# Block attention and two expert layers on one core: lookup tables built on the chip, and a new hand-written order of all steps

## The chip, the core and the metric

The kernel runs on one core of a Trainium2 chip. The metric is the time of one execution in microseconds (us), taken on the device. Engines are named as the profile names them: PE is the matrix engine, PEld its weight load, DVE the vector engine, ACT the scalar (activation) engine, POOL the GpSimd engine, and SP the engine on whose queue all transfers from and to memory are issued.

## What is computed

```python
# attention: q, k, v of shape (2, 8, 768, 64); block = 32, window = 16
k_sum = k.reshape(B, H, nb, block, D).max(axis=3)
v_sum = v.reshape(B, H, nb, block, D).mean(axis=3)
scores_l = scale * np.matmul(q, k.transpose(0, 1, 3, 2))        # kept where |i - j| < window, else -1e9
scores_s = scale * np.einsum('bhsd,bhnd->bhsn', q, k_sum) + np.log(block)
a = softmax(concatenate([scores_l_masked, scores_s]))            # 768 local + 24 block columns
attn = np.matmul(a, concatenate([v, v_sum]))
# x: (1536, 512), two expert layers with d_ff = 2048
h = x @ w_in;  g = h * np.clip(h + 3.0, 0.0, 6.0) / 6.0;  x = g @ w_out
h = x @ w2_in; out = (h * sigmoid(h)) @ w2_out
```

## The kernel before, in words

The 1536 tokens are two batches of 768. **Attention** works in 24 units, two for each of 12 groups of 128 queries. For a group, `scores` multiplies 64-row windows of q with 96 local keys and the 24 block maxima; `masked` (DVE) adds the mask table and takes the row minimum; `exps` and `guard` (ACT) make the exponentials and their sum; `inverse` (DVE) and `normal` (POOL or DVE) divide; `turn` (PE) transposes and `turned` (ACT or DVE) copies out; `mix` (PE) multiplies with a window of v that `load_v` brings from memory and whose last 24 rows `v_put` fills with block means; `mixed_hi` and `mixed_lo` split the result into two parts x = hi + lo. Before that, `load` brings k, q and v; `par` (first batch of k) sorts token parity, `tr` transposes on PE against the identity matrix `ident`, `k_copy`, `q_copy` and `k_max` take the result out of PSUM, and `keys` (POOL or DVE) lays out the window of keys. The block maxima span a whole batch, so no score of a batch can be made before all k of it has come; the block means likewise need all v of a batch.

**The expert layers** keep the precision of float32 by splitting both operands in two float32r parts and making three products. A weight tile of 128 rows is brought by `fetch` (512 KB, the first half of a pair w_in, the second w_out) and split by `conv_top` (ACT or DVE), `conv_join` (DVE), `conv_hi` (ACT or DVE) and `conv_lo` (POOL or DVE). `hidden i p` is half a step of the first product (6 matmuls of 512 columns, `p` is 0 or 1), `act`, `gate`, `gate_hi`, `gate_lo` make the activation and its two parts, and `project i p` is half a step of the second product. The first 24 steps of `hidden` work on blocks of 512 tokens; the very first block is tokens 0 to 511, which are attention groups 0 to 3 (units 0 to 7). Later steps use sums of products (`prod`, `prodb`, `ssum`, `tsum`, `c11` and the like), which save PE work and cost DVE work.

**The order** is one written table, `ORDER`: 1961 entries that are issued in this order, each on the engine of its function, so that each engine has a fixed list that it works through without overtaking. A `*` behind an entry puts a copy or subtraction on DVE that would otherwise be on ACT or POOL (`copier`, and `eng` in `normal`, `keys`, `conv_lo`). Buffers are taken from rings in the order of the table. `rouse` and `warm` are matmuls whose results nobody reads; they lie in the gaps of PE in the first microseconds.

The table `cst` holds the identity matrix (128 columns), a matrix for the block means (48 columns) and three masks (360 columns). Before, the host makes it in `shape_constants`, and `table 0` and `table 1` (line 1177) bring it from memory in two transfers of 88 and 180 KB. It is used by `tr` and `turn` (L500, L675), `v_sums` (L551), `v_rows` (L566) and `masked` (L633). Lines that the prediction speaks of: `fetch` L416 and L418, `load` L458 and L473, `par` L486, `scores` L618, `exps` L647, `normal` L667, `mix` L689, `mixed_hi` L711, `mixed_lo` L715, `hidden` L731, first-layer `project` L808. In the changed kernel these lines are 14 less.

## Time and profile before

| what | value |
|---|---|
| median of 3 runs (lowest to highest) | 586.29 us (584.81 to 587.84) |
| the profiled execution's own time | 586.36 us |
| its span in the profile | 584.6 us |
| granted PE clock over the span | 0.997 of full |
| busy over the span: PE, DVE, ACT, POOL | 97%, 79%, 45%, 14% |
| moved from and to memory | 47.81 MB read, 3.15 MB written |

How to read it: the span is measured from the first instruction to the last, and the profiled execution's own time has 1.8 us around it. Matmuls are pipelined and their ends are modelled, so the start of one to the start of the next says how long it held PE, and a busy share of PE is not a share of useful work. All engines work through their lists in order, so a wait of one instruction holds back everything behind it on that engine.

### The profile page before, as it was taken

To read this page: it belongs to the slowest core of one execution; us is meant where nothing else is said; L and a number is where in the kernel's file an instruction comes from. 1 tells how busy PE (TensorE), PEld (TensorE's weight loads), DVE (VectorE), ACT (ScalarE), POOL (GpSimd) and SP (SyncE) were. 2 spreads that over 40 slices of the span, in tenths; PEclk is the share of its full clock that TensorE was granted. 3 is DMA by queue.
4 is the path that set the end of the run, shared out by engine and by line. 5 is a ranking of instruction groups with operands and counts; after the bars stand their busy time and mean duration, and the time that the engine had idled before them with its cause. 6 is when DMAs were issued, how large, how long until landed. Compare 5 with 4: busy or idle time off the path is not lost.

```text
span 584.6 us, 9610 instructions
## 1 busy us (share of the span) xinstructions
PE 569.9 (97%) x3624; PEld 481.0 (82%) x3624; DVE 460.9 (79%) x1033; ACT 263.3 (45%) x614; POOL 81.1 (14%) x88
## 2 busy tenths in 40 slices
PE   8789999999999999999999999999999999999997
PEld 7677788888888888888888887888888898888886
DVE  3699986687749898998999999748987686757764
ACT  4797784544142416243446474524445134424220
POOL 1253314140001100001100402002010000111000
PEclk9998999999999999999999999999999999999999
DMA  9998896222001103224121111131322211220013
GB/s 225 237 213 211 222 247 168 64 43 83 36 1 36 40 33 109 72 76 139 39 73 36 37 36 43 67 108 50 94 73 81 100 37 36 73 61 13 0 73 144
DMA packets 70094, 51.57 MB, mean 88 GB/s; under 512 B 38432, under 2 KB 64544, under 8 KB 70048
## 3 DMA queue, kind: packets, MB, share of 16 engines
q1 hardware_dynamic: 70048, 50.97, 32.4%
q8 instruction: 28, 0.46, 0.3%
q14 instruction: 18, 0.15, 0.1%
HBM read 47.81 MB, written 3.15 MB: 87 GB/s over the span
## 4 chain that ended last, share of the span: by engine, by line
PE 85%; DVE 8%; DMA 2%; ACT 2%; SPq 1%; issue 1%; POOL 0%; DVEq 0%; POOLq 0%
PE bank L1035 26%; PE bank L808 23%; PE bank L811 21%; PE bank L731 10%; PE bank L689 2%; DMA stage<-in_v_dram 1%; PE bank L675 1%; PE bank L618 1%; DMA early_w<-in_q_dram 1%; DVE r L1082 1%; DVE bits L435 1%; SPq L458 1%; DVE values L1082 1%; SPq L473 1%; ACT early_units L647 1%
## 5 line engine op out<-in xcount | busy, mean ns | idle before, releaser
L808 PE MATMUL bank<-g,w 128*128 128x512 f32 x432 | 105.5, 392 | 0.0
L811 PE MATMUL bank<-w,g 128*128 128x512 f32 (+1 forms) x429 | 101.2, 385 | 0.0
L808 PEld LDWEIGHTS bank<-g,w 128*128 128x128 f32 x432 | 79.9, 188 | 16.4 <-issue 0.4
L811 PEld LDWEIGHTS bank<-w,g 128*128 128x128 f32 x429 | 79.5, 188 | 16.0
L450 POOL TENSOR_TENSOR w<-bits,w 128x512 fp32r<-128x512 f32 x25 | 36.2, 1454 | 288.0 <-ACT w L446 216.4
L1035 PE MATMUL bank<-w,x 128*128 128x512 f32 (+1 forms) x360 | 74.2, 348 | 0.9 <-DVE x L1018 0.6
L1035 PEld LDWEIGHTS bank<-w,x 128*128 128x128 f32 x360 | 59.2, 189 | 10.4 <-DVE r L1060 0.8
L1035 PE MATMUL bank<-x,w 128*128 128x512 f32 (+1 forms) x240 | 49.4, 348 | 0.0
L731 PE MATMUL bank<-x,w 128*128 128x512 f32 x192 | 46.8, 395 | 0.5 <-DVE stat L633 0.5
L1035 PEld LDWEIGHTS bank<-x,w 128*128 128x128 f32 x240 | 39.3, 189 | 5.8
L731 PEld LDWEIGHTS bank<-x,w 128*128 128x128 f32 x192 | 35.4, 188 | 8.5 <-DVE stat L633 0.9
L426 ACT CAST top<-words 128x512 f16<-128x512 bf16 x46 | 35.8, 778 | 12.6 <-DVE cst L435 3.7
L435 DVE SCALAR_TENSOR_TENSOR bits<-words,top 128x512 uint32<-128x512 uint32 x49 | 36.0, 734 | 4.9 <-ACT top L426 4.0
L762 ACT ACTIVATE values<-values 128x512 f32<-128x512 f32 x39 | 24.3, 627 | 34.0 <-DVE values L1076 20.0
L811 PE MATMUL bank<-w,w 128*128 128x512 f32 (+1 forms) x159 | 39.4, 386 | 0.0
L788 DVE TENSOR_TENSOR g<-values,g 128x512 fp32r<-128x512 f32 x46 | 31.6, 686 | 7.1 <-ACT g L782 6.5
L808 PE MATMUL bank<-w,w 128*128 128x512 f32 x144 | 36.5, 391 | 0.0
L811 PEld LDWEIGHTS bank<-w,w 128*128 128x128 f32 x159 | 29.4, 188 | 5.8
L808 PEld LDWEIGHTS bank<-w,w 128*128 128x128 f32 x144 | 26.8, 188 | 5.4
L1035 PE MATMUL bank<-w,w 128*128 128x256 f32 (+1 forms) x144 | 28.5, 337 | 0.7 <-DVE r L1082 0.7
L446 ACT CAST w<-bits 128x512 fp32r<-128x512 f32 x30 | 18.5, 620 | 22.6 <-DVE bits L435 14.7
L1082 DVE TENSOR_TENSOR values<-bank,values 128x512 f32<-128x512 f32 x37 | 25.3, 687 | 3.3 <-PE bank L1035 2.4
(193 smaller groups left out, 971.5 us busy)
## 6 DMA issues: line engine op xcount, KB each, us to landing
words<-in_moe_w_out_dram SPq DMA_DIRECT2D x32, 511.8 KB, 3.3
words<-in_moe_w_in_dram SPq DMA_DIRECT2D x32, 511.0 KB, 3.8
early_w<-in_q_dram SPq DMA_DIRECT2D x12, 256.0 KB, 5.3
out_dram<-acc SPq DMA_DIRECT2D x11, 256.0 KB, 2.0
early_r<-in_v_dram SPq DMA_DIRECT2D x13, 192.0 KB, 4.5
stage<-in_k_dram SPq DMA_DIRECT2D x3, 512.0 KB, 5.2
stage<-in_v_dram SPq DMA_DIRECT2D x3, 512.0 KB, 7.4
early_w<-in_k_dram SPq DMA_DIRECT2D x6, 256.0 KB, 5.6
```

Of the source, the lines that this page charges most:

```text
L426: copier("conv_top", h)(out=top[:, 1], in_=src[:, 2])
L435: nc.vector.scalar_tensor_tensor(out=bitss.take(h, bit_users(h)), in0=rest, scalar=13, in1=tops.use(h).bitcast(U32), op0=ALU.logical_shift ...
L446: copier("conv_hi", h)(out=w_half(h, 0), in_=bitss.use(h).bitcast(F32))
L450: eng.tensor_tensor(out=w_half(h, 1), in0=bitss.use(h).bitcast(F32), in1=w_half(h, 0).bitcast(F32), op=ALU.subtract,)
L689: nc.tensor.matmul(ps[D * e : D * e + D, o : o + QW], v[:NSLOT, h * D : (h + 1) * D], own(pTs, 2 * n + e)[:NSLOT, hp * P + QW * w : hp * P ...
L731: nc.tensor.matmul(ps[:, :n], w[:, a, kk * P : (kk + 1) * P], x[:, o // SUB : (o + n) // SUB, b, kk, :], start=(m == 0), stop=(m == last),)
L762: nc.scalar.activation(out=r, in_=ps, **kind)
L788: eng.tensor_tensor(out=g[:, 1, cols], in0=r[:, cols], in1=g[:, 0, cols].bitcast(F32), op=ALU.subtract)
L808: nc.tensor.matmul(ps[:, o : o + n], lhs, g[:, b, shift : shift + n], **flags)
L811: nc.tensor.matmul(ps[:, : len(cols)], g[:, a, rows], rhs, **flags)
L1035: nc.tensor.matmul(ps, lhs(a, kk), rhs(b, kk), start=(i == 0), stop=(i == 5))
L1082: nc.vector.tensor_tensor(out=out, in0=banks.use(("prod", p, k)), in1=r, op=ALU.add)
```

## The change

Three things change. The two transfers of the table are gone; the host's table is a single zero that nobody reads. In their place POOL makes the table with three new steps: `diagonal` (a memset and an affine select), `masks` (a memset, two affine selects, two copies, three memsets) and `means` (a memset, two affine selects). And the table `ORDER` is another one: 1962 entries, the same steps with the same counts apart from the tables, in another order, with 213 instead of 195 entries marked `*`.

```diff
-    c[:, :P] = np.eye(P)
-    c[np.arange(P), Z0 + 16 + np.arange(P) // 16] = 1.0 / BLOCK
-    return c
+    return np.zeros((1, 1), np.float32)
...
 ORDER = """
-zero, grow 6, grow 9, rouse 6, rouse 11, rouse 5, rouse 9, load k 0 0, par k 0 1, rouse 4, table 0, rouse 10,
+zero, rouse 11, rouse 3, load k 0 0, par k 0 0, rouse 8, rouse 5, rouse 10, clear, load k 0 2, rouse 1,
...
-    def table(part):
-        cols = slice(0, M0) if part == 0 else slice(M0, NCONST)
-        nc.sync.dma_start(out=cst[:, cols], in_=consts[:, cols])
+    def diagonal():
+        nc.gpsimd.memset(ident, 0.0)
+        nc.gpsimd.affine_select(
+            out=ident,
+            in_=ident,
+            compare_op=ALU.not_equal,
+            fill=1.0,
...
+    def band(t, expr, base, sign, fill):
+
+        nc.gpsimd.affine_select(
+            out=t, in_=t, compare_op=ALU.is_ge, fill=fill, base=base, pattern=expr,
+            channel_multiplier=sign,
+        )
+
+    def means():
+
+        t = cst[:, Z0:M0]
+        nc.gpsimd.memset(t, 1.0 / BLOCK)
+        band(t, [[-16, M0 - Z0]], 256, 1, 0.0)
+        band(t, [[16, M0 - Z0]], -241, -1, 0.0)
+
+    def masks():
+
+        wide = kws[0][:, : LOC + QW]
+        nc.gpsimd.memset(wide, 0.0)
+        band(wide, [[1, LOC + QW]], -1, -1, -1e9)
+        band(wide, [[-1, LOC + QW]], 2 * WINDOW - 1, 1, -1e9)
+        view = cst[:, M0:].rearrange("p (m n) -> p m n", m=3)
+        for rows, o in ((slice(0, QW), 0), (slice(QW, P), QW)):
+            nc.gpsimd.tensor_copy(
+                out=view[rows, :, :LOC],
+                in_=wide[rows, o : o + LOC].unsqueeze(1).to_broadcast([QW, 3, LOC]),
+            )
+        nc.gpsimd.memset(view[:QW, 0, :PAD], -1e9)
+        nc.gpsimd.memset(view[QW:, 2, LOC - PAD : LOC], -1e9)
+        nc.gpsimd.memset(view[:, :, LOC:], math.log(BLOCK))
```

**The start of SP's queue.** Names: `stage` takes k and v of the first batch, `early_w` with `in_q_dram` or `in_k_dram` a quarter of a batch's q or k, `cst` the table, `words` a weight tile. Before:

```order
L458 DMA stage_80<-in_k_dram 128x8x128
L1177 DMA cst<-in_consts_dram 128x176
L458 DMA stage_81<-in_k_dram 128x8x128
L458 DMA stage_82<-in_k_dram 128x8x128
L473 DMA early_w_88<-in_q_dram 128x8x64 x2
L1177 DMA cst<-in_consts_dram 128x360
L473 DMA early_w_88<-in_q_dram 128x8x64 x2
L458 DMA stage_83<-in_v_dram 128x8x128
L473 DMA early_w_88<-in_k_dram 128x8x64 x2
L458 DMA stage_83<-in_v_dram 128x8x128
L458 DMA stage_84<-in_v_dram 128x8x128
```

and now:

```order
L444 DMA stage_80<-in_k_dram 128x8x128
L444 DMA stage_81<-in_k_dram 128x8x128
L444 DMA stage_82<-in_k_dram 128x8x128
L459 DMA early_w_88<-in_q_dram 128x8x64 x4
L444 DMA stage_83<-in_v_dram 128x8x128 x2
L444 DMA stage_84<-in_v_dram 128x8x128
L459 DMA early_w_88<-in_k_dram 128x8x64 x2
L402 DMA words_69<-in_moe_w_in_dram 128x4x511
L404 DMA words_70<-in_moe_w_out_dram 128x2047
L459 DMA early_w_88<-in_q_dram 128x8x64 x2
```

The two transfers of the table are gone, and the first transfer of the second batch's k stands behind all three of v instead of behind the first.

**PE around the first `hidden`.** The tiles `x_0` are the first 512 tokens, `bank` with `cst` on the right a transposition (`tr` or `turn`), `early_g`/`early_units`/`early_r` on the right alone a `mix`. Before, from the last row of one `scores` of a later group (the last `mix` of the first 512 tokens stands ten rows ahead of it):

```order
L618 MATMUL bank_74<-early_units,early_w_89 64x120 x2
L731 MATMUL bank_75<-x_0_64,w_87 128x512 x12
L500 MATMUL bank_76<-cst,early_w_88 128x128 x4
L675 MATMUL bank_79<-cst,early_units 120x128 x4
L500 MATMUL bank_72<-cst,early_w_88 128x128 x4
L731 MATMUL bank_78<-x_0_64,w_441 128x512 x12
L731 MATMUL bank_73<-x_0_64,w_442 128x512 x12
```

and now:

```order
L675 MATMUL bank_78<-early_g_96,early_r_97 64x64 x16
L486 MATMUL bank_77<-cst,early_w_88 128x128 x4
L717 MATMUL bank_76<-x_0_64,w_87 128x512 x6
L717 MATMUL bank_73<-x_0_64,w_86 128x512 x12
L486 MATMUL bank_72<-cst,early_w_88 128x128 x4
L486 MATMUL bank_75<-cst,early_w_88 128x128 x4
L717 MATMUL bank_76<-x_0_64,w_87 128x512 x6
L486 MATMUL bank_79<-cst,early_w_88 128x128 x4
L486 MATMUL bank_78<-cst,early_w_88 128x128 x4
L717 MATMUL bank_74<-x_0_64,w_327 128x512 x6
```

Now the first `hidden` stands directly behind one transposition after the last `mix`, and the second batch's first transpositions, which stood ahead of it, stand between the halves of the next ones.

**POOL's start.** `top`, `kT` and `early_r` are cleared first in both; `cst` is the table, and `ISA` with the line of the next instruction is a reload of POOL's library. Now:

```order
L1227 MEMSET early_r_97 96x512
L1162 MEMSET cst 128x128
L1163 ISA
L1163 AFFINE_SELECT cst<-cst 128x128
L1190 MEMSET early_w_95 128x160
L1175 AFFINE_SELECT early_w_95<-early_w_95 128x160 x2
L1195 COPY cst<-early_w_95 64x3x96 x2
L1199 MEMSET cst 64x16
L1200 MEMSET cst 64x16
L1201 MEMSET cst 128x3x24
L579 COPY early_w_95<-kT_98 128x4x96
```

Before, the copy of `keys` (L593) followed the clearing of `early_r` at once, and the reload stood ahead of the first `normal` (L667).

## Rows read from the trace of the kernel before

**Rows 1.** Page of the profile: busy us, share of the span, number of instructions.

```profile
PE 569.9 (97%) x3624; PEld 481.0 (82%) x3624; DVE 460.9 (79%) x1033; ACT 263.3 (45%) x614; POOL 81.1 (14%) x88
```

**Rows 2.** Timeline of PE, 44 to 110 us: start, duration, line, out<-in, [idle before <-releaser].

```profile
45.56 1.71 PE L618 MATMUL bank<-early_w,early_w 64*64 64x120 f32 x32 [1.34 <-DVE early_w L527]
...
48.24 1.57 PE L689 MATMUL bank<-early_g,early_r 120*64 120x64 f32 x32
...
50.33 1.05 PE L618 MATMUL bank<-early_units,early_w 64*64 64x120 f32 x32
51.31 3.02 PE L731 MATMUL bank<-x,w 128*128 128x512 f32 x12
54.17 0.60 PE L500 MATMUL bank<-cst,early_w 128*128 128x128 f32 x4
54.60 0.60 PE L675 MATMUL bank<-cst,early_units 128*120 128x128 f32 x4
...
58.85 3.04 PE L731 MATMUL bank<-x,w 128*128 128x512 f32 x12 [0.45 <-DVE stat L633]
...
67.37 1.15 PE L689 MATMUL bank<-early_units 120*64 120x64 f32 x32
68.46 3.01 PE L808 MATMUL bank<-g,w 128*128 128x512 f32 x12
...
77.16 5.62 PE L731 MATMUL bank<-x,w 128*128 128x512 f32 x24
```

**Rows 3.** Chain of waits, whole span: start, duration, what it went through.

```profile
250.15 16.32 PE bank L808 x72
```

**Rows 4.** Waits of PE after 100 us: us in total, times, longest.

```profile
PE bank L1035 <- DVE r L1082: 0.7, 1, 0.7
PE bank L1035 <- DVE x L1018: 0.6, 1, 0.6
```

**Rows 5.** Chain of waits followed back from 60 us: start, duration, what it went through.

```profile
0.74 0.42 SPq L458
...
5.06 6.12 DMA early_w<-in_q_dram
...
15.66 7.51 DMA stage<-in_v_dram
...
25.37 0.58 ACT early_units L576
...
28.02 1.53 ACT early_units L647 x8
...
29.56 0.21 ACT stat L658
...
36.64 0.20 DVE early_units L633
...
37.25 0.60 DVE kmax L514
...
49.87 0.59 ACT x L711
...
50.48 0.69 DVE x L715
```

**Rows 6.** Stretches of 10 us: stretch, length, busy us (instructions) by engine, PE clock, DMA share, GB/s.

```profile
30.00:40.00 10.00, 8.50 (x164) 7.31 (x162) 9.16 (x48) 9.88 (x39) 5.16 (x7) 1.00 1.15 196
40.00:50.00 10.00, 8.43 (x130) 6.96 (x127) 9.14 (x31) 7.90 (x38) 8.05 (x15) 0.83 1.08 251
50.00:60.00 10.00, 9.55 (x77) 7.64 (x76) 9.41 (x39) 7.71 (x27) 0.00 (x0) 1.00 0.81 204
```

**Rows 7.** Timeline of POOL, 0 to 40 us: start, duration, instruction, [idle before <-releaser].

```profile
1.46 0.52 POOL L1203 MEMSET early_r<- 96x512 f32 x1
11.96 0.50 POOL L593 COPY early_w<-kT 128x384 f32<-128x384 f32 x1 [9.97 <-ACT kT L508]
...
24.45 0.99 POOL L667 TENSOR_TENSOR early_units<-early_units,stat 128x480 f32<-128x480 f32 x1 [0.70 <-DVE stat L662]
```

More of the change, by code (lines that the diff above doesn't have):

```diff
@@ L153 @@
-q_copy 1 2 1, conv_hi 9, load_v 14, mix 6, scores 9, keys 21, turn 17, mixed_hi 6, turned 17, conv_lo 7*,
-load_v 15, gate_lo 3, project 3 0, conv_top 12*, conv_join 12, project 3 1, grow 0, conv_hi 12, mixed_lo 6,
-masked 19, exps 19, mix 7, mixed_hi 7, conv_lo 12, mixed_lo 7, hidden 6 0, keys 20, fetch 13, conv_top 13*,
-hidden 6 1, conv_join 13, load_v 16, gate_hi 5*, conv_hi 13*, normal 16, turn 16, turned 16*, conv_lo 13*,
-guard 19, hidden 14 0, inverse 19, normal 19*, hidden 14 1, fetch 14, conv_top 14, conv_join 14, conv_hi 14*,
@@ L158 @@
-gate_hi 4, gate_lo 4, masked 18, load_v 17, act 6, hidden 11 0, hidden 11 1, act 11, fetch 11, conv_top 11,
-act 14, project 2 1, gate 6, gate 11, turn 19, mix 8, conv_lo 14, fetch 15, gate 14, exps 18, conv_join 11,
-fetch 19, scores 10, keys 22*, conv_top 15*, gate_lo 5, guard 18, conv_lo 9, project 4 0, load_v 19,
-inverse 18, turned 19, normal 18, mixed_hi 8, load_v 18, mixed_lo 8, masked 21, hidden 13 0, gate_hi 6*,
-hidden 13 1, act 13, conv_join 15, gate 13, grow 5, turn 18, turned 18*, gate_lo 6, exps 21, guard 21,
@@ new lines @@
+masked 10, mixed_lo 0, load_v 6, turned 7, masked 11, keys 9, turned 5*, grow 9, load_v 7, keys 8, scores 4,
+exps 10, masked 9, turn 4, conv_lo 1, mix 3, turned 4, masked 8, load_v 5, mixed_lo 1, mixed_hi 3, mixed_lo 3,
+load_v 4, mix 2, mixed_hi 2, mixed_lo 2, tr k 1 2 0, conv_lo 2, hidden 1 0, conv_top 6*, conv_join 6,
+guard 10, conv_hi 6*, exps 8, guard 8, fetch 4, conv_top 4*, conv_join 4, conv_hi 4*, exps 11, guard 11,
+conv_lo 6*, inverse 10, inverse 8, load k 1 1, conv_lo 4*, exps 9, hidden 0 0, hidden 0 1, normal 10,
@@ new lines @@
+v_sums 1 0, gate_hi 0*, load_v 10, tr q 1 1 0, exps 12, tr q 1 1 1, turn 9, gate_hi 2*, guard 12, hidden 3 0,
+hidden 3 1, masked 13, keys 16, turned 9, fetch 5, gate_lo 0, gate_lo 1, conv_lo 3*, q_copy 1 1 0, exps 13,
+inverse 12, normal 12*, load v 1 2, normal 11, guard 13, project 0 0, load v 1 1, grow 1, inverse 13,
+normal 13, act 3, gate 3, turn 11, fetch 7, turned 11*, q_copy 1 1 1, conv_top 5, conv_join 5, masked 15,
+project 1 0, turn 12, scores 8, masked 14, turn 13, masked 16, masked 17, v_pair 1 1, project 0 1, exps 15,
@@ new lines @@
+project 2 1, gate_lo 4, turn 17, turned 17, scores 9, keys 20*, masked 19, masked 18, exps 19, load_v 17,
+keys 21*, mix 7, mixed_hi 7*, load_v 16, mix 8, conv_lo 12, exps 18, hidden 6 0, hidden 6 1, guard 18,
+mixed_lo 7, hidden 10 0, mixed_hi 8*, guard 19, hidden 10 1, act 6, inverse 18, normal 18*, gate 6,
+mixed_lo 8, act 10, gate 10, hidden 11 0, hidden 11 1, conv_hi 9, conv_lo 9*, inverse 19, act 11, gate 11,
+grow 0, turn 18, gate_hi 6*, normal 19, gate_lo 6, fetch 13, conv_top 13, project 4 0, conv_join 13,
@@ new lines @@
+conv_hi 13*, fetch 14, conv_top 14*, turn 19, turned 19, scores 10, masked 20, exps 20, conv_lo 13*,
+hidden 14 0, hidden 14 1, masked 21, exps 21, conv_join 14, guard 20, keys 22*, project 4 1, conv_hi 14*,
+act 14, conv_lo 14*, guard 21, keys 23, inverse 20, fetch 11, conv_top 11*, normal 20*, conv_join 11,
+conv_hi 11, gate 14, hidden 13 0, gate_hi 5, gate_lo 5, hidden 7 0, hidden 7 1, act 7, load_v 18, inverse 21,
+hidden 13 1, project 6 0, conv_lo 11, gate 7, act 13, gate 13, fetch 15, turned 18, load_v 19, mix 9,
@@ new lines @@
+load_v 21, conv_top 15*, turn 20, turned 20, normal 21, scores 11, hidden 8 0, grow 2, project 6 1,
+mixed_hi 9*, masked 22, exps 22, conv_join 15, conv_hi 15*, conv_lo 15, gate_hi 7, gate_lo 7, gate_hi 10,
+turn 21, guard 22, turned 21*, tsum 0 3 0, mixed_lo 9, project 5 0, project 7 0, hidden 12 0, hidden 12 1,
+hidden 8 1, inverse 22, masked 23, exps 23, guard 23, load_v 20, normal 22, hidden 15 0, t_hi 0 3 0,
+t_lo 0 3 0, act 8, gate 8, finish 0 0 0 0, mix 10, load_v 23, mixed_hi 10, mixed_lo 10, hidden 15 1,
```

395 lines of the change are left out of this document (187 added, 208 removed).

## Prediction

> **What bounds the kernel now.** I read the page first: PE is busy 97% of the span and every other engine less than 80% [rows 1]. So the end moves only with microseconds in which PE does nothing useful, and the next question is where those are. The timeline of PE answers it. The first `hidden` starts at 51.31 us, and from there matmuls follow one another with few gaps, such as 0.45 us ahead of 58.85 [rows 2]; after 100 us the waits of PE that the trace names are a few of 0.4 to 0.7 us [rows 4]. The reader should see that from about 77 us on there is next to nothing to win, and that the start is where PE time is lost.
>
> How much is lost there comes from counting. The price of a PE step is its start to the next start: a half step of `hidden` or `project` 1.36 us (72 matmuls in 16.32, so 6 in 1.36 [rows 3]), a transposition (`tr`, `turn`) 0.43 to 0.44, `scores` 0.98, `mix` 1.09 [rows 2]. Ahead of the first `hidden` the order of before has 20 `tr`, 11 `turn`, 8 `scores`, 4 `mix` and the sums over v (2.8 us, the same in both kernels): 31 x 0.44 + 8 x 0.98 + 4 x 1.09 + 2.8 = 28.6 us of useful work. It starts at 51.3, so **22.7 us are lost**. At 77.16, when step 4 of `hidden` starts, the useful work ahead of it is 53.5 us by the same prices (28.6, then 14 half steps, 7 turns, 4 `tr`, 2 `mix` and so on), so the loss has grown to 23.7. `rouse` and `warm` count as loss. The rest of the loss is a few microseconds up to the end, and the tail (the last products and their stores) stands in the same order in both.
>
> What sets 51.3? The chain of waits shows it: transfers until 23.2 us (q until 11.2, the last v until 15.66 + 7.51 = 23.17), then ACT and DVE in turn until `mixed_hi` at 49.87 and `mixed_lo` at 50.48 [rows 5]. The stretches agree: from 30 to 60 us DVE is busy 9.1 to 9.4 of 10 us and ACT 7.7 to 9.9 [rows 6]. **The start is bound by transfers for about 23 us and by ACT and DVE after that.**
>
> **The change, part by part. The transfers.** The table is 0.27 MB. The last v is the end of 4.99 MB in the order of before and came at 23.17, so 4.99 / (23.17 - 0.74) = 0.222 MB per us, with 0.74 the first issue [rows 5]. Now 4.19 MB stand up to the last v: 19.6 us. But PE's list has the second batch's first k next, before `scores 3` of the first; it is the end of 4.72 MB, 22.0 us. PE then needs two `tr` halves, the row of block means and a `turn` before `scores 3`, about 2.4 us: 24.4, against the 25.37 at which ACT's chain behind the same point started [rows 5]. Gain at this point: **about 1 us**. Up to the last window of v that the first 512 tokens need, the queue holds 9.40 MB instead of 9.68: weights (2 MB) and the second batch's k are still ahead, so what is named as being put off is put off by little. At 0.222 that is 43.1 us instead of 44.3, no later than ACT needs.
>
> **ACT up to the first `hidden`.** This term sets the start. First the method on the kernel before: from 25.37 [rows 5] to its last `mixed_hi` of the first 512 tokens ACT has 8 `exps` (1.53), 7 `guard` (0.2), 16 copies (0.58) and 2 `conv_top` (0.75): 12.2 + 1.4 + 9.3 + 1.5 = 24.4, which gives 49.8; it ended at 49.87 + 0.59 = 50.5. So ACT ran with 0.7 us of waits. Now: q's second quarter is transposed at 22.9, its copy ends at 23.5, an `exps` and a `guard` end at 25.2, and then come 6 `exps`, 5 `guard`, 15 copies, 1 `conv_top`: 9.2 + 1.0 + 8.7 + 0.75 = 19.65. That is 44.9; with the same 0.7 of waits 45.6, and `mixed_lo` (0.6 to the next issue [rows 5]) makes 46.2. DVE has 17 us in that time and is no bound, and POOL 12. **The first `hidden` starts near 46.2 instead of 51.3.** But the work ahead of it on PE is less as well: 16 `tr`, 8 `turn`, 6 `scores`, 4 `mix`, the v sums: 23.6 us. Loss: 46.2 - 23.6 = **22.6, against 22.7**. Five microseconds earlier, with five microseconds of work put off: by itself it gains nothing.
>
> **What was put off.** From the first `hidden` to step 4 PE now has 57.6 - 23.6 = 34.0 us of work, DVE 32.9 and ACT 29.7 by the prices above (before: 24.9, 18.9, 18.4). All is nearly in balance, so PE is not covered with ease. I walked it: the three halves of `hidden` to 50.3, the second batch's `tr` (their q can be issued only when a k buffer is free, at about 46, and lands near 50), step 2 at 53.5 (its `conv_lo` ends on POOL near 51), two `scores` near 57 to 59 behind a key copy of ACT that ends near 56.5, `project 0` at 63.5 behind `gate_lo` at 63.3, step 1 of it 0.4 late behind `conv_lo` on DVE, step 4 at 80.1 to 81. Loss there: 22.5 to 23.4, I take 22.9, against 23.7: **-0.8 us**.
>
> **The tables on POOL.** 13 short instructions. No row shows an affine select; the nearest rows bound one between 0 and the 0.99 of a 480-column multiplication, and a 512-column memset took 0.52 [rows 7]; I take 0.3, nearest the memset for 128 and 160 columns. Ten stand ahead of the first `keys`, at most 9.9 us from 1.98, so 11.9; POOL was idle until 11.96 before [rows 7], and `masked` needs the masks after 14. The identity is two of them, at most 2.0, so ready by 4.0, ahead of the first transposition (near 7, after k has landed and been sorted). Cover: POOL's idle time, of which even the upper price uses no more than there was. **0**. What it costs if the cover is gone is a rival below.
>
> The reload of POOL's library now stands ahead of the first affine select. Before, it stood ahead of the first `normal` at 24.45, which waited 0.70 us, by the profile for DVE, and took 0.99 [rows 7]: a reload cost at most 0.7 us there. [...]
>
> **After 80 us.** Entries on DVE grow by 12.5 us over the kernel by these prices, ACT falls by 12.5, POOL by 6. DVE was busy 79% [rows 1], and PE's named waits are all for DVE [rows 4]. Bounds: the stalls left there, 1.3 us in the two longest rows and perhaps 3 in all, go (-3), or DVE's added work falls half on the path (+6). I take 0, as the order is fitted to its own list both times, and keep the ends for the range.
>
> **Sum:** 586.36 - 0.8 + 0 + 0 = 585.6, say 585.5 for the profiled execution, which stands 0.07 above the median of 586.29. Half a percent, 2.9 us, is what a measurement here can tell from none.
>
> **The rivals. A: a front without its stalls, faster.** [...] If ACT runs without waits, the first `hidden` starts at 45.5 and the loss is 21.9; if PE keeps that to step 4, it is 1.8 under the 23.7 of before; with the clock up another 1.5: 583. With the later stalls gone as well, 580 or a little less. For it: less is asked of ACT and DVE ahead of the first `hidden`. Against: PE has more gaps, not fewer, before it. 0.32.
>
> **B: DVE becomes the bound behind the first `hidden`, slower.** The mechanism is the balance above: 32.9 us of DVE work against 34.0 of PE between the first `hidden` and step 4, with copies on ACT, keys on POOL and transfers between them. Each wait of DVE over 1.1 us in all goes to PE. In 50 to 60 DVE lost 0.6 us of 10 even when full [rows 6]; at that rate 34 us lose 2, and waits for late second-batch transfers 2 to 3 more. With some of the 12.5 us later, 4 to 7 us: 590 to 593. It decides where `project 0` starts after 66 or step 4 after 84. 0.28.
>
> **C: POOL's first table instruction waits behind the reload.** The identity is needed near 7 and would be there by 4 at the upper price, so the wait decides from 3 us on, four times the 0.70 of the row [rows 7]; each further microsecond starts the transpositions later, until q's landing at about 11 [rows 5] hides it. With 1 to 1.5 us on the path: 587, inside no change. [...] 0.06.
>
> **D: the change does little of what it says.** That is my forecast, in effect: 9.40 against 9.68 MB ahead of the last load needed. 0.34.
>
> **How the numbers follow.** The forecast D with C is no change within 0.5%, 0.40; A faster by over 0.5%, 0.32; B slower by over 0.5%, 0.28. The range runs from A with the later stalls gone to B with 6 to 7 us: 578.5 to 592.5; the likeliest case alone spans 583.4 to 589.2.
>
> **What would show it.** First `hidden` at 45 to 48 us; last v near 20; the identity ready before 5 and PE not waiting for POOL; `project 0` at 63 to 65, step 4 at 80 to 82; PE's waits after 100 us below 4. Wrong if the first `hidden` comes after 49 or before 44, if DVE idles in 46 to 80 while PE waits on it, or if new PE waits of over 1 us appear after 100.

## The result, and the profile after

The changed kernel takes **593.87 us** (median of 4 runs, 593.04 to 595.22) beside 585.55 for the kernel before on the same chip: a ratio of **1.0128, 95% interval 1.011 to 1.0146**. It is slower, by 8.3 us between the two medians and by 7.5 us by the ratio, where no change was forecast, and it lies above the range's upper end of 592.5.

The page of the changed kernel, busy time of the whole span:

```profile
span 592.1 us, 9608 instructions
PE 573.3 (97%) x3624; PEld 482.8 (82%) x3624; DVE 475.6 (80%) x1056; ACT 254.4 (43%) x597; POOL 76.8 (13%) x95
```

PE runs the same 3624 matmuls as before [rows 1], DVE has 14.7 us more and ACT 8.9 less. The span of the profiled execution is 7.5 us longer (592.1 against 584.6). To see where, count the big matmuls (512 columns, one of 256 as a half) in PE's records of the profiled execution and note when the n-th starts. At each of these five marks the same number of small matmuls stands ahead in both kernels, so that the starts can be compared:

| matmul no. | before | changed | difference |
|---|---|---|---|
| 200 | 114.97 | 116.93 | +1.96 |
| 400 | 167.01 | 169.23 | +2.22 |
| 800 | 258.37 | 262.12 | +3.75 |
| 1100 | 328.03 | 336.34 | +8.31 |
| 2000 | 536.22 | 543.56 | +7.34 |

So there are two losses: **about 2 us at the start, and about 6 us between 170 and 336 us**, for which the prediction put nothing into its sum; behind that the changed list wins back 1 us.

The start. PE in order of time, the start and length of a group, and in brackets the idle time before it with what ended it:

```profile
16.68 0.61 PE L604 MATMUL bank<-kmax,early_w 64*64 64x24 f32 x32
17.22 0.64 PE L537 MATMUL bank<-stage,cst 128*32 128x128 f32 x15
20.83 1.67 PE L537 MATMUL bank<-stage,cst 128*32 128x128 f32 x33 [2.98 <-issue]
22.43 1.23 PE L1219 MATMUL bank<-early_w 128*128 128x128 f32 x4
23.45 2.12 PE L486 MATMUL bank<-cst,early_w 128*128 128x128 f32 x12
...
27.08 1.05 PE L604 MATMUL bank<-early_units,early_w 64*64 64x120 f32 x32
...
48.55 0.50 PE L717 MATMUL bank<-x,w 128*128 128x512 f32 x1
...
66.62 1.52 PE L794 MATMUL bank<-g,w 128*128 128x512 f32 x6
...
83.23 2.89 PE L717 MATMUL bank<-x,w 128*128 128x512 f32 x12
```

`v_sums` (L537) stops for 2.98 us, ended by "issue", that is by nothing the profile shows. Behind it a dummy step of four matmuls takes 1.23 us and twelve passes of transposition 2.12, where eleven took 1.42 in the kernel before:

```profile
19.65 1.42 PE L500 MATMUL bank<-cst,early_w 128*128 128x128 f32 x11 [2.09 <-DMA early_w<-in_k_dram]
```

The stretches of the changed kernel say why (columns: stretch and its length; busy time and instructions of PE, PEld, DVE, ACT, POOL; then PE's granted clock, DMA share, GB/s):

```profile
20.00:30.00 10.00, 8.51 (x103) 7.19 (x104) 5.40 (x26) 5.42 (x25) 2.91 (x6) 0.83 0.74 190
30.00:40.00 10.00, 7.45 (x98) 6.07 (x97) 8.02 (x38) 9.77 (x43) 6.29 (x7) 0.75 1.13 214
40.00:50.00 10.00, 9.62 (x177) 7.99 (x174) 8.54 (x42) 8.67 (x30) 5.27 (x7) 0.91 0.87 192
```

Before, only one of these stretches was below full clock, that from 40 to 50 [rows 6]; from 20 to 30 us its row reads:

```profile
20.00:30.00 10.00, 8.45 (x152) 6.90 (x151) 7.03 (x29) 7.35 (x27) 3.79 (x9) 1.00 0.98 221
```

Here all three are below it: in the profile's record of the granted clock PE stood at 0.5 of full from 21.4 to 24.8 us, after the wait of 2.98, and again from 35.0 to 41.8, within and behind a wait of 1.64 us, with two of 0.6 to 0.7 before it. ACT and DVE, busy 5.4 of 10 us, stood for the same thing: ACT waited 4.45 us for the second quarter of q. `scores 3` came at 27.08, the first `hidden` at 48.55, step 4 at 83.23.

What the first of the two stretches at half clock cost can be read from a later run, "gates ahead" below, whose list is the same up to the late part and which was granted the full clock, 1.00, from 20 to 30 us:

```profile
21.60 1.17 PE L539 MATMUL bank<-stage,cst 128*32 128x128 f32 x33 [3.02 <-issue]
26.22 1.05 PE L606 MATMUL bank<-early_units,early_w 64*64 64x120 f32 x32
```

From the end of the stop to `scores 3` it takes 4.62 us, the changed kernel 6.25 (27.08 - 20.83). So that stretch cost 1.6 us. The stop itself was as long in both, 3.0 us; a stop of this length was followed by the lower clock in one execution and not in the other.

The late loss. PE has three waits of over 1 us after 100 us: 1.16 at 240.20, 3.45 at 305.83 and 1.82 at 324.64, each from start to start less a matmul. First PE, then ACT, then DVE, around the longest:

```profile
304.70 1.52 PE L1021 MATMUL bank<-w,x 128*128 128x512 f32 x6
309.51 1.67 PE L1021 MATMUL bank<-w,w 128*128 128x512 f32 x6 [3.29 <-DVE r L1068]
...
324.64 0.39 PE L794 MATMUL bank<-g,w 128*128 128x512 f32 x1
326.69 1.65 PE L794 MATMUL bank<-g,w 128*128 128x512 f32 x6 [1.66 <-DVE g L774]
```

```profile
299.23 0.76 ACT L412 CAST top<-words 128x512 f16<-128x512 bf16 x1
306.25 0.40 ACT L1000 CAST x<-words 128x256 fp32r<-128x256 f32 x1 [6.26 <-PE bank L1021]
306.57 0.62 ACT L748 ACTIVATE values<-r 128x512 f32<-128x512 f32 x1
```

```profile
300.71 0.42 DVE L990 TENSOR_TENSOR words<-cst,bits 128x256 f32<-128x256 f32 x1
307.22 0.69 DVE L759 SCALAR_TENSOR_TENSOR r<-values,r 128x512 f32<-128x512 f32 x1 [6.09 <-ACT values L748]
307.83 0.68 DVE L421 SCALAR_TENSOR_TENSOR cst<-words,top 128x512 uint32<-128x512 uint32 x1
308.43 0.42 DVE L1004 TENSOR_TENSOR x<-words,x 128x256 fp32r<-128x256 f32 x1
308.77 0.68 DVE L1068 TENSOR_TENSOR r<-bank,r 128x512 f32<-128x512 f32 x1
```

Read them from the bottom up. PE's next step, `prod 7 4`, needs a PSUM bank, which `c11 7` (DVE, 308.77) frees. On DVE `c11 7` stands behind `gate 39` (307.22), which waits 6.09 us for `act 39` on ACT (306.57). `act 39` stands behind `s_hi 8 2` (306.25), and that waits 6.26 us: it writes the split sums of step 8 into the only buffer for them, which `prod 7 5` on PE reads until 306.22 (304.70 + 1.52). So for 6 us ACT and DVE stand idle for PE, and then PE stands 3.29 us for the way back. In the old list `s_hi 8 2` stands 67 entries behind `prod 7 5`, here right behind it. After 310 DVE is full (14.93 us busy of 15), and a second wait follows at 324.64. Before, the longest named waits after 100 us were 0.7 and 0.6 us [rows 4].

### The profile page after: what moved, and what is told of

Its sections match the earlier page's. It is cut to its first block, busy times and chain, and to the rows that moved or that the text cites. A ratio compares the mean times of both kernels' runs of the same rounds, so it can differ in the third digit from the quotient of the medians.

```text
span 592.1 us, 9608 instructions
## 1 busy us (share of the span) xinstructions
PE 573.3 (97%) x3624; PEld 482.8 (82%) x3624; DVE 475.6 (80%) x1056; ACT 254.4 (43%) x597; POOL 76.8 (13%) x95
## 4 chain that ended last, share of the span: by engine, by line
PE 55%; DVE 3%; issue 0%; ACT 0%
PE bank L1021 25%; PE bank L797 22%; PE bank L794 8%; DVE values L1068 0%; DVE g L774 0%; DVE acc L843 0%; DVE values L950 0%; DVE x L881 0%; DVE r L759 0%; DVE bits L421 0%; DVE r L1068 0%; DVE w L774 0%; DVE x L1004 0%; DVE cst L421 0%; DVE x L967 0%
## 5 line engine op out<-in xcount | busy, mean ns | idle before, releaser
L797 PE MATMUL bank<-w,g 128*128 128x512 f32 (+1 forms) x453 | 105.9, 386 | 0.0
L797 PEld LDWEIGHTS bank<-w,g 128*128 128x128 f32 x453 | 83.7, 188 | 17.2 <-DVE values L1068 0.4
L436 POOL TENSOR_TENSOR w<-bits,w 128x512 fp32r<-128x512 f32 x22 | 30.0, 1369 | 267.4 <-ACT w L432 115.8
L717 PE MATMUL bank<-x,w 128*128 128x512 f32 x192 | 48.1, 398 | 0.3 <-DVE x L701 0.2
L774 DVE TENSOR_TENSOR g<-values,g 128x512 fp32r<-128x512 f32 x46 | 34.0, 740 | 6.6 <-ACT g L768 6.0
L1068 DVE TENSOR_TENSOR values<-bank,values 128x512 f32<-128x512 f32 x45 | 30.8, 686 | 7.4 <-PE bank L1021 6.7
L412 ACT CAST top<-words 128x512 f16<-128x512 bf16 x39 | 30.2, 775 | 11.1 <-DVE bits L421 7.5
L797 PE MATMUL bank<-w,w 128*128 128x512 f32 (+1 forms) x135 | 32.6, 384 | 0.0
L768 ACT CAST g<-values 128x512 fp32r<-128x512 f32 x32 | 19.7, 620 | 29.1 <-PE bank L797 15.7
L794 PEld LDWEIGHTS bank<-w,w 128*128 128x128 f32 x144 | 26.8, 188 | 5.5
L797 PEld LDWEIGHTS bank<-w,w 128*128 128x128 f32 x135 | 25.0, 188 | 5.0
```

The costliest lines, as they stand in the source:

```text
L412: copier("conv_top", h)(out=top[:, 1], in_=src[:, 2])
L436: eng.tensor_tensor(out=w_half(h, 1), in0=bitss.use(h).bitcast(F32), in1=w_half(h, 0).bitcast(F32), op=ALU.subtract,)
L717: nc.tensor.matmul(ps[:, :n], w[:, a, kk * P : (kk + 1) * P], x[:, o // SUB : (o + n) // SUB, b, kk, :], start=(m == 0), stop=(m == last),)
L768: copier("gate_hi", i)(out=g[:, 0, cols], in_=value(i)[:, cols])
L774: eng.tensor_tensor(out=g[:, 1, cols], in0=r[:, cols], in1=g[:, 0, cols].bitcast(F32), op=ALU.subtract)
L794: nc.tensor.matmul(ps[:, o : o + n], lhs, g[:, b, shift : shift + n], **flags)
```

## The experiments

Times are medians, each with its ratio to the kernel before and the 95% interval. The kernel before ran beside each of them, with medians from 586.08 to 586.42, so the ratios compare better than the times. Line numbers in the experiments are 2 or 3 higher than in the changed kernel.

### The late stall

**Splits of step 8 moved behind the way back.**

```diff
-prod 7 5, s_hi 8 2, act 39, gate 39, conv_join 35, s_lo 8 2, c11 7, s_hi 8 4*, gate_hi 38, vee 7, s_hi 8 3,
-gate_hi 39, gate_lo 38, prod 7 4, gate_lo 39,
+prod 7 5, act 39, gate 39, conv_join 35, c11 7, gate_hi 38, vee 7,
+gate_hi 39, gate_lo 38, prod 7 4, gate_lo 39, s_hi 8 2, s_lo 8 2, s_hi 8 4*, s_hi 8 3,
```

> The changed kernel with one edit to its list: the four steps that split the sums of bag 8 of the gradient (s_hi 8 2, s_lo 8 2, s_hi 8 4, s_hi 8 3) stand behind gate_lo 39 and so behind prod 7 4. Theory T1, a turn-around: in the changed kernel ACT waits at s_hi 8 2 for the one buffer of sums that prod 7 5 still reads, c11 7 stands behind it on DVE, and prod 7 4 on PE waits for c11 7; so PE loses 3.45 us at 305.8 and, because DVE never catches up, 1.8 us more at 324.6. By T1 both stalls are gone and the time falls by 3.5 to 5.3 us, from 593.9 to 588.6 to 590.4. Rival T2, DVE overloaded: DVE has 12.5 us more to do than before and is the bound in this stretch, so the stall only comes back within 30 us of the old place, PE loses as much in sum, and the time stays at 592 to 594.

Measured: **590.89 us** (1.0092, 1.0068 to 1.0116), 3.0 less than the changed kernel by the medians and 2.1 by the ratios, whose intervals just overlap; it lies between the times of T1 and T2. PE goes through without a gap, and from no. 400 to no. 1100 of the big matmuls it takes 163.3 us instead of 167.1:

```profile
303.96 1.52 PE L1023 MATMUL bank<-w,x 128*128 128x512 f32 x6
305.32 1.52 PE L1023 MATMUL bank<-w,w 128*128 128x512 f32 x6
306.68 1.52 PE L796 MATMUL bank<-w,w 128*128 128x512 f32 x6
```

T1 holds for the stall of 3.45 us and fails for the second wait, which stays, at 320.28, with 1.66 us. Four other kernels here keep these entries in place; like the changed one, each has the stall, at 304 to 310 us and with 3.447 to 3.452 us, whatever its start. It belongs to the list and not to lateness.

**All old engines behind `hidden 4 0`.** As above, and from there each entry carries the `*` it had before, for example:

```diff
-u2b 5*, finish 0 0 2 3, prodb 5 7, gate 25, veeb 5,
+u2b 5, finish 0 0 2 3, prodb 5 7, gate 25, veeb 5*,
```

> The changed kernel with the four splits of bag 8 moved (the run that took 590.89), and for every entry after hidden 4 0 the engine that it had in the kernel before (the marks for DVE), the order unchanged. Theory: what is left of the late loss, 1.15 us at 239.5 and 1.66 at 320.3, stands where DVE is full (its gate is done late, ACT waits for DVE), and DVE has 12.5 us more to do in the changed list than before; with the old engines these two waits fall below 0.5 each and the time falls by 2 to 3 us, to 588 to 589. Rival: the list was fitted to its own engines, so ACT becomes late where it was not, new waits of PE over 1 us appear, 591 to 595.

Measured: **597.37 us** (1.0194, 1.0173 to 1.0215). The theory falls: new waits come where the new list had none of this size.

```profile
PE bank L488 <- ACT early_units L564: 1.7, 1, 1.7
PE bank L719 <- ACT early_g L668: 1.4, 1, 1.4
PE bank L677 <- DMA early_r<-in_v_dram: 1.0, 1, 1.0
```

These are the waits of PE from 80 to 130 us (sum, times, longest). The new order with the old engines is 6.5 us worse than with its own, so the 12 us more on DVE are not a fault one can take out by itself.

**Eleven steps off DVE in two stretches.**

```diff
-vee 4*, conv_lo 20*,
+vee 4, conv_lo 20,
...
-u2b 5*,
+u2b 5,
...
-conv_hi 23*,
+conv_hi 23,
```

and in the same way `conv_top 34`, `s_hi 7 1`, `gate_hi 36`, `c21b 7`, `s_hi 8 4`, `c21 7` and `conv_top 37`.

> The changed kernel with the splits of bag 8 moved (590.89), and 11 steps of two stretches (from vee 4 to conv_hi 23, and from conv_top 34 to conv_top 37) off DVE, on the engine that the kernel before had for them; all other steps as in the changed kernel. The run with all old engines took 597.4, because new waits came at 86 to 123 and 410 us, while the wait at 240 was gone and that at 320 fell from 1.66 to 1.19. Theory: in these two stretches DVE is full and its 0.6 us a step is what the gates wait for; the waits at 239.5 and 320.3 fall below 0.5 each and the time to 588 to 589.5. Rival: the steps are as late on ACT, or the wait moves on by some 20 us; 590.5 to 592.

Measured: **590.89 us** (1.0068, 1.0051 to 1.0084), the same median as without it; by the ratios 0.24% less, with intervals that overlap. The wait near 240 fell from 1.15 to 0.78 us, that near 322 from 1.66 to 1.57. The time is the rival's, and what is left of the waits says that it is not load alone.

**Gates ahead of steps that nobody waits for.**

```diff
-gate_hi 32*, gate_lo 32, prod 5 3, conv_lo 23*, gate_hi 26, conv_join 26, project 24 1, project 25 1, gate_lo 26,
+gate_hi 26, gate_lo 26, gate_hi 32*, gate_lo 32, prod 5 3, conv_lo 23*, conv_join 26, project 24 1, project 25 1,
...
-gate_hi 47, project 46 0, conv_hi 35, finish_lo 2 0, conv_top 37*, gate_hi 45, act 43, project 46 1,
-finish_lo 2 2, gate_lo 47, gate_lo 45,
+gate_hi 47, gate_hi 45, gate_lo 47, gate_lo 45, project 46 0, conv_hi 35, finish_lo 2 0, conv_top 37*, act 43,
+project 46 1, finish_lo 2 2,
```

> The changed kernel with the splits of bag 8 moved (590.89) and five gate steps earlier in the list, engines unchanged: gate_hi 26 and gate_lo 26 ahead of gate_hi 32, and gate_hi 45, gate_lo 47, gate_lo 45 right behind gate_hi 47. Taking 11 steps off DVE left the wait at 322 at 1.57 us and the time at 590.89, so load alone is not it. Theory P, place: at 239.5 and 320.3 PE waits for a gate_lo whose gate_hi ACT had done 3 to 4 us before (235.9 and 317.1) and that stands on DVE behind four to six steps nobody waits for. With the gates ahead of these the two waits fall below 0.4 us each and the time to 588 to 589. Rival: the steps that are now later are wanted too (sums of bag 8, conversions of the next weights), a wait of the same size comes within 10 us, 590 to 591.5.

Measured: **590.83 us** (1.0072, 1.0045 to 1.0099), its six runs spread from 588.85 to 593.05. In the profile the theory holds in the main. The waits of PE from 230 to 330 us, first with the splits alone moved, then with the gates too:

```profile
PE bank L796 <- DVE g L776: 2.5, 2, 1.5
```

```profile
PE bank L796 <- DVE g L776: 0.8, 2, 0.5
```

1.7 us of named waits are gone. From no. 400 to no. 1100 this kernel takes 162.2 us, 1.1 less than with the splits alone (163.3); the kernel before takes 161.0, the changed one 167.1. The time does not settle it: the intervals of the two ratios overlap, and the six runs, with mean granted clocks from 0.991 to 0.997, spread over 4.2 us.

### The halves exchanged

**The tables alone**, in the list of the kernel before:

```diff
-rouse 4, table 0, rouse 10,
+rouse 4, diagonal, rouse 10,
...
-keys 5, k_copy 0 2 1, table 1, q_copy 0 0 1,
+masks, keys 5, k_copy 0 2 1, q_copy 0 0 1,
...
-v_sums 0 0,
+means, v_sums 0 0,
```

> The kernel before, its list and the order of its loads kept, with the two tables built on GpSimd instead of loaded (diagonal where the first table's load stood, masks ahead of keys 5, means ahead of v_sums 0 0). Theory: the tables cost nothing and the two loads that fall away free 0 to 1 us of the input's landing; first hidden within 1 us of the kernel before's (45.9) and the time 584.5 to 586. [...]

Measured: **585.19 us** (0.9984, 0.9973 to 0.9995), 0.9 less than the kernel before. The tables are not part of the loss.

**The new list up to `hidden 4 0`, the old one behind it.** The seam, after 374 entries of the new list:

```diff
 project 3 1, conv_hi 10*, load_v 12,
-hidden 4 0, load_v 13, conv_lo 10*, hidden 4 1, act 4, v_put 1 2*,
+keys 18*, turn 14, hidden 4 0, hidden 4 1, exps 17, guard 17, conv_lo 10*,
```

> The changed kernel's list up to hidden 4 0 (its first 374 entries), every later entry in the order of the kernel before. By the sum of the two traces the start costs +2 us (step 4 of the projections at 83.2 instead of 81) and the rest of the list +5.3 us by its own stalls at 305.8 and 324.6. So this kernel stands at 587 to 588.5, and no wait of PE after 100 us is above 1.2 us. Rival: the late stalls come from the late start or from any misfit between list and machine, not from the changed list's later part: then new stalls of over 2 us show after 80 us and the time is 591 to 595.

Measured: **592.56 us** (1.0111, 1.0077 to 1.0146), 589.14 to 594.01. PE's longest gap after 100 us is 0.91 us, so the late stalls do belong to the later list; but the time is the rival's. In the profiled execution, the fastest of the four at 589.14, no. 200 of the big matmuls starts at 118.00 and no. 2000 at 539.24, both 3.0 us later than before: all that it loses is lost in the first 118 us.

**The old start, the new list behind it.** The seam, after 351 entries of the old list with the new tables:

```diff
 conv_hi 8*, load q 1 2, conv_lo 8*,
-hidden 4 0, hidden 4 1, inverse 15, conv_top 10*, conv_join 10,
+gate_hi 2*, inverse 15, normal 15, conv_top 7, conv_join 7,
```

> The other half of the exchange: up to hidden 4 0 the list of the kernel before with the tables built on GpSimd (the start of the kernel that took 585.19), after that the changed list. If the late part alone costs its own stalls (3.45, 1.8 and 1.2 us at 305.8, 324.6 and 240.2, less 2.5 of the older list's), the time is 585.2 + 4 to 5.3 = 589 to 590.5 with the same three waits in PE's row. If the changed start alone is what costs (592.56 with the old later list, +7.4 on 585.19), the late stalls are in part slack that a late start has used up, and the time is 585 to 588.

Measured: **597.99 us** (1.0185, 1.014 to 1.0229), a miss for both sides. The stall of 3.45 us is there, at 310.4, and at 78.3 a new one:

```profile
PE bank L796 <- DVE w L776: 2.9, 1, 2.9
```

Late in both waits PE's granted clock fell to 0.5 of full, from 80.7 to 87.6 and from 312.8 to 319.7 us; at the late stall of the changed kernel it did not.

The halves cost +7.4 and +12.8 us over the 585.19 of the old list with new tables, both together +8.7. Such parts don't add: the second seam makes a wait of its own, the clock differs, and the two runs can't price a half.

### The start

**Dummy matmuls ahead of `v_sums 0 1`.**

```diff
 v_sums 0 0, keys 4, k_copy 0 2 1, load v 0 2, load v 0 1,
+rouse 12, rouse 13, rouse 14, rouse 15, rouse 16, rouse 17,
 v_sums 0 1,
```

> The changed kernel with six more of the dummy 128x512 products (rouse 12 to 17) ahead of v_sums 0 1, so that PE has something to do in the 2.98 us in which it waits for the landing of v at 17.8 to 20.8 us. Theory: the half clock of 21.4 to 24.8 us comes behind this wait, so it is gone, scores 3 stands 1.2 to 1.7 us earlier than at 27.08, and the time falls by as much, from 593.9 to 592.2 to 592.7. Rival: the first 49 us are bound by ACT's copies and DVE's sums behind the landing, whatever PE's clock is; then the first hidden stays within 0.4 us of 48.55 and the time at 593.5 to 594.3. A gain of over 3 us would say that the half clock held up more than the steps that ran in it.

Measured: **597.65 us** (1.0216, 1.0182 to 1.0249). The edit did not do what it was made for, and that was the find:

```profile
20.51 0.30 PE L540 MATMUL bank<-stage,cst 128*32 128x128 f32 x1 [1.94 <-issue]
20.73 2.94 PE L1222 MATMUL bank<-early_w 128*128 128x128 f32 x24
```

The dummies, which wait for no landing, ran behind the wait too, and so did the last matmul of `v_sums 0 0`, whose v had landed by 15.2 us in the changed kernel. PE stands after 223 matmuls in every kernel with this start and nothing added ahead of it, and goes on 1.3 to 1.6 us after a packet of 16 KB on the queue named "instruction" has come (18.15 + 1.21, then 20.83 in the changed kernel), in all eleven of their traces.

**Tiny matmuls ahead of `par k 1 1`**, where PE stands for 1.39 us from start to start until k has been sorted. Theory F takes the stop for PE having run out of its own program; if that is so, more instructions ahead of it bring the packet of 16 KB earlier.

```diff
+    def fill(i):
+        ps = banks.take(("fill", i), 1)
+        for _ in range(10):
+            nc.tensor.matmul(ps[:8, :8], vsum[:, :8], vsum[:, :8], start=True, stop=True)
+        banks.use(("fill", i))
...
 load k 0 1, masks,
+fill 0, fill 1,
 par k 1 1,
```

> The changed kernel with 20 tiny products (8x8, 40 passes of TensorE) put ahead of par k 1 1, where PE waits 1.39 us for the landing of k (8.7 to 10.1 us). In the changed kernel PE stands from 17.86 to 20.83 us with nothing to wait for in its list: all of v had landed by 18.88, and the pass at which it stands is number 222 in the changed kernel and in the two kernels with the same start, whatever follows; in that gap a 16 KB packet of PE's own program lands (18.15 to 19.36). Theory F: PE ran out of program, because the packet is asked for at a certain pass and stands behind the loads. With 40 passes more before it, the packet is asked for some 4 us earlier and the wait is gone: v_sums 0 1 by 18.5, all three v_sums done by 19.5, the q of the second quarter transposed by 21.5 to 22.5 instead of 25.5, and the time falls by 2 to 4 us, to 590 to 592. Rival L, a landing or a buffer: PE goes on at 20.8 as before, 593 to 595.

Measured: **593.33 us** (1.0126, 1.0103 to 1.0149). DMA queues and issues from 18 to 20 us in the changed kernel, where the packet of 16 KB (queue q8) lies in the wait:

```profile
q1 hardware_dynamic: 1786, 0.46, 125.9%
q8 instruction: 1, 0.02, 3.8%
```

and from 12 to 13.5 us with the tiny matmuls, with the last load of v, then PE:

```profile
q8 instruction: 1, 0.02, 5.5%
...
stage<-in_v_dram SPq DMA_DIRECT2D x1, 512.0 KB, 8.4
```

```profile
17.19 0.64 PE L539 MATMUL bank<-stage,cst 128*32 128x128 f32 x16
20.30 1.25 PE L539 MATMUL bank<-stage,cst 128*32 128x128 f32 x32 [2.46 <-DMA stage<-in_v_dram]
```

The packet came 6 us earlier, all 16 matmuls of `v_sums 0 0` ran without a stop, and "issue" is gone: theory F holds for the cause of the stop, as far as this run can show it. But v landed later, at 16.7, 18.5 and 20.25 us instead of 15.2, 17.1 and 18.9: the load that landed at 11.8 was not later, the next one, at 14.9 instead of 13.4, and all of v behind it were, so the delay begins where the 16 KB now stood. A landing took the place of the wait. The gain is 0.5 us at 20.3, and the time is the rival's.

**The same with the old later list**: `fill 0, fill 1` ahead of `par k 1 1` in the kernel with the first seam above.

> The tiny products of the run before in the kernel with the changed start and the later list of the kernel before (the one that took 592.56). By theory F the start gains 2 to 4 us here too, because nothing late eats it: 588 to 590.5; the wait of PE ahead of v_sums 0 1 is gone. By rival L 592 to 593. If the wait is gone and the time still 592 to 593, the start is bound elsewhere than at PE.

Measured: **590.27 us** (1.0071, 1.0045 to 1.0097), inside F's numbers, though its profile shows v as the bound as above and the intervals of the pair overlap (592.56 without).

**The second quarter of q ahead of v.**

```diff
+tr q 0 1 1, tr q 0 1 0,
 v_sums 0 0, keys 4, k_copy 0 2 1, load v 0 2, load v 0 1, v_sums 0 1, v_sums 0 2,
...
-rouse 7, tr q 0 1 1, masked 2, tr k 1 0 0, v_add 0, tr q 0 1 0, exps 0,
+rouse 7, masked 2, tr k 1 0 0, exps 0,
...
-v_rows 0, fetch 1,
+v_add 0, v_rows 0, fetch 1,
...
-turn 3, load q 0 2,
+scores 3, turn 3, load q 0 2,
...
-conv_top 0*, scores 3, keys 10,
+conv_top 0*, keys 10,
```

> The changed kernel with the second quarter of q transposed ahead of v_sums 0 0 (on PE at 17.2 us, before the pass at which PE runs out of program) instead of behind v_sums 0 2; v_add 0 on DVE behind q_copy 0 1 1, and scores 3 ahead of turn 3. The q of this quarter had landed by 13.5 us. Theory: the start of the changed kernel is late because PE, ACT and DVE all stand for v (PE 2.98 us, ACT 4.45, DVE 3.0) while q lies ready: ACT copies q at 21.0 instead of 25.6, scores 3 comes at 23 to 24.5 instead of 27.1, the first hidden at 45.5 to 46.5 instead of 48.55, and the time falls by 2 to 3 us, to 591 to 592. Rival: from scores 3 on the sum of ACT's work sets the first hidden, and ACT had other work to wait for (k of the second batch, 22.4): the first hidden stays within 0.7 of 48.55 and the time at 593 to 594.

Measured: **593.52 us** (1.0117, 1.0088 to 1.0147). The first `hidden` came at 47.14, 1.4 us earlier; the time did not move clear of noise. In the profiled execution no. 2000 of the big matmuls is 1.0 us earlier, although here the late stall is followed by 0.5 of full clock from 308.3 to 311.7 us, and the six matmuls behind it take 2.72 us instead of 1.67: here the stall cost more than its own length. The same edit in the kernel with the first seam:

> The same start as in the run with q first, followed by the later list of the kernel before (with the changed start as it was this took 592.56). If q first gains 2 to 3 us at the start, this kernel gains as much, because the older later list has no stall that eats it: 589 to 591. If it takes under 585.2 (the older list with the tables built on GpSimd) the changed start is the better one after this repair; at 591 to 593 q first gains nothing.

Measured: **588.94 us** (1.0044, 1.0027 to 1.0061), 3.6 less than without, and the intervals are apart. Its ten runs stand apart by the mean granted clock listed with each: 587.3 to 588.3 us at 0.997, 588.8 to 589.9 at 0.994, 590.2 and 591.1 at 0.991. So do those of the old list with new tables: 583.7 to 584.0 at 1.000, 585.2 to 585.6 at 0.996 and 0.997. **0.003 of the mean clock goes with about 1.4 us** (the means of these groups lie 1.4 to 1.5 apart), which fits the 1.6 us read above for one stretch at half clock: 3.4 us at half clock are 0.003 of the mean over 590 us.

**Gates, splits and q first together**, and the same **with dummies in PE's waits**:

```diff
+rouse 12,
 turn 2,
...
+rouse 13,
 tr q 0 2 0,
...
+rouse 14, rouse 15, rouse 16,
 turn 1,
```

> The run before together with the start that transposes the second quarter of q first (alone 593.52: the first hidden came 1.4 us earlier, and 0.35 less at the changed kernel's 593.87 is within the spread). If the late stalls are what ate that gain, both together save the sum: the time of the run before less 0.5 to 1.5, 586.5 to 588.5. If the start's gain is eaten by the clock or by work put off, the time equals the run before within 0.4.

> The kernel of the run before with five dummy steps (rouse, four passes each, about 0.5 us) put where PE waits at 28 to 36 us: one ahead of turn 2 (wait of 0.77 us), one ahead of tr q 0 2 0 (0.61), three ahead of turn 1 (1.61). Theory C, clock: by 80 us PE idles 9.4 us in the changed kernel and 9.8 in the kernel before, but stands at the lower clock for 10.2 us of it instead of 3.4, which is the 2.2 us that the start costs; over the runs of one kernel 0.003 less of the mean granted clock goes with 1.3 to 1.4 us. With PE busy in these waits the stretch at half clock of 35 to 42 us goes, the mean granted clock rises by 0.003 to 0.006 over the run before, and the time falls by 1 to 2.5 us. Rival: the clock falls all the same, because PE is idle elsewhere, or the dummies push the work behind them; then the time is the same or up to 1.5 us longer.

Measured: **588.54 us** (1.0031, 1.0018 to 1.0044) and **587.88 us** (1.0033, 1.0016 to 1.005). The first is 2.3 us below the run without q first, more than expected. One reading is that the start counts once the late stalls are out; the two profiled executions, with spans of 587.0 and 587.1 us, don't show it. With the dummies the mean clock is at 1.000 in 6 of 10 runs instead of 1 of 10, and in the profiled one the clock is full all through the start:

```profile
20.00:30.00 10.00, 8.47 (x145) 7.08 (x145) 7.83 (x37) 7.73 (x35) 3.48 (x7) 1.00 1.00 243
30.00:40.00 10.00, 8.39 (x136) 7.24 (x135) 7.11 (x32) 9.80 (x38) 7.49 (x7) 1.00 1.25 209
40.00:50.00 10.00, 9.10 (x127) 7.25 (x126) 9.72 (x45) 9.18 (x40) 3.48 (x6) 1.00 1.08 230
```

The first `hidden` is at 45.38 there and at 47.12 without the dummies. But `scores 3` is earlier by as much already (23.94 and 25.70), ahead of the first dummy at 25.85: the run without them had a stretch at half clock from 21.4 us, which the dummies could not touch. So this pair of profiles does not price them. Theory C is borne out by the count of runs at full clock; of the 1 to 2.5 us 0.7 showed in the medians and nothing in the ratios.

**Dummies in the waits of the old list with new tables:**

```diff
+rouse 12,
 turn 1,
...
+rouse 13, rouse 14,
 turn 7,
...
+rouse 15, rouse 16,
 scores 6,
```

> The kernel before's list with the tables built on GpSimd (585.19) and five dummy steps (rouse) where its PE waits: one ahead of turn 1 (0.89 us at 28.0), two ahead of turn 7 (1.30 at 31.2), two ahead of scores 6 (1.32 at 43.3). Of this kernel's ten runs without them three had a mean granted clock of 1.000 and took 583.7 to 584.0, seven had 0.996 or 0.997 and took 585.2 to 585.6. Theory C, clock: with the dummies nearly all runs have 1.000, and the median is 583.7 to 584.3. Rival: the clock is as before, or the dummies cost what they gain: 585 to 586. What only a later result could tell: whether it beats both kernels, 586.3 and 593.9.

Measured: **585.34 us** (0.9983, 0.9972 to 0.9994). The clock is at 1.000 in 8 of 12 runs instead of 3 of 10, but such a run now takes 585.0 to 586.2 instead of 583.7 to 584.0. The rival holds: the dummies cost what they gain. The old list with the tables built on POOL, with or without dummies, is the only version ahead of both kernels, by 0.16 to 0.17%.

## Why the prediction was wrong

**Right: the transfers.** Last v was put at 19.6 us and landed at 18.88, the first k of the second batch at 22.0 and landed at 21.37 and 22.41.

**Wrong: what PE does with them.** "24.4" for `scores 3` took PE to be free when the data is there; it came at 27.08. PE stood from 17.86 to 20.83 in the stop named "issue", which theory F puts down to PE's program and which was gone with the tiny matmuls. The old list waited 2.09 us for k here anyway, up to 19.65, so that nothing in the rows of before showed it. Then PE ran at half clock to 24.8. The second quarter of q was copied at 25.61 instead of 22.9. Of the 2.7 us by which `scores 3` was late, 1.6 are the lower clock, as read above, and 1.1 are left for the stop.

**Right: the walk from there.** From q's copy to the first `hidden` the prediction has 46.2 - 22.9 = 23.3 us, measured 48.55 - 25.61 = 22.9; from the first `hidden` to step 4 it has 33.9 to 34.8, measured 34.7. So the loss at step 4 is 83.23 - 57.6 = 25.6 us, not 22.9; against the 23.7 of before a term put at -0.8 came out at +1.9. The miss of 2.7 us was there before 27 us and only carried along. The list behind the 53.5 us of work ("14 half steps, 7 turns, 4 `tr`") is wrong: PE's records have 12 half steps, 4 `turn` and 2 `tr` from 51.31 to 77.16. Recounted by the same prices both losses are 0.8 to 0.9 higher, and their difference, 1.9 to 2.0, stays.

**Right: the tables, cost 0.** An affine select took 0.29 us, as estimated, and two wider ones 0.70 together; the identity stood at 2.56 (2.27 + 0.29). The first affine select began 0.08 us after the memset before it:

```profile
1.99 0.20 POOL L1162 MEMSET cst<- 128x128 f32 x1
2.27 0.29 POOL L1163 TENSOR_SCALAR_AFFINE_SELECT cst<-cst 128x128 f32<-128x128 f32 x1
2.50 0.23 POOL L1190 MEMSET early_w<- 128x160 f32 x1
2.80 0.70 POOL L1175 TENSOR_SCALAR_AFFINE_SELECT early_w<-early_w 128x160 f32<-128x160 f32 x2
```

Rival C falls with that.

**Wrong: "After 80 us: 0", the step that cost most.** It was taken because "the order is fitted to its own list both times". Measured: +5.5 us by the span (7.5 less the 2.0 that stood at the 200th big matmul), near the upper bound of 6 that was kept. Of it 3.45 us are one place, shown by moving four entries. The two other waits, 1.16 and 1.82 us, stand at gates placed late on DVE: moving these gave 1.1 us in PE's records, which the times don't settle. The rest of the list gives about 1 us back. The bound looked at DVE's load; what cost most was the place of steps in fixed lists. The prediction's own sign, new waits of PE over 1 us after 100, came true three times.

**Rival B** had the right side and a right test (`project 0` after 66: it came at 66.62), but not the mechanism: between the first `hidden` and step 4 PE was full (30.00 us busy of 30 from 50 to 80), and the only wait for DVE that the profile names there is 0.22 us at 49.27. **D**, the forecast, fell with the two steps above; **A** needed fewer gaps at the start, and there were longer ones at a lower clock. No run shows its 1.5 us for the clock as such. In the trace of before the granted clock is 0.5 of full from 45.80 to 49.21 us; the `scores` and the `mix` that ran there took 0.66 and 0.42 us more than the others of [rows 2], and a turn 1.11 us beside 0.65. In the changed kernel a stretch of the same length cost 1.6 us.

Open: repaired in all places named, the changed list takes 588.54, and 587.88 with dummies: 5.3 to 6.0 us are back. By the ratios 0.3%, about 1.9 us, stay. The lower clock is not all of it: between the two lists with dummies, the new one repaired and the old one with new tables, whose profiled executions both have a mean clock of 1.000, no. 200 differs by 0.9 us (114.76 and 113.88) and no. 2000 by 1.8 (536.90 and 535.13). So half of the rest stands in the start and half behind it; its cause was not tried.

## What to carry to other kernels

In fixed lists look for a step that takes the only copy of a buffer from another engine while that engine's next step hangs, over one or two lists, on work queued behind it: here one such entry cost 3.45 us with both helper engines idle for 6 us in front of it. A new order of a whole list can bring such a place in, and here its engines or its halves could not be exchanged for the old ones without new waits. Here an idle stretch of PE cost again in the clock afterwards (1.6 us behind a stop of 3.0, and not in every execution), so an earlier first step of the main work is worth little when it is bought with longer waits.
